# Pooled-attention kernel with adapters: key loads across 128 partitions and spread over the loop, first queries turned on TensorE, logits left in place, Exp without a bias tile

## The chip, the cores and the metric

The kernel runs on one core of one Trainium2 chip. The metric is the device time of one execution in microseconds (us). Times are medians of several executions, with the lowest and highest beside them. A run counts as slow when it is over 1.5% above the fastest of the same kernel. Ratios are the mean time of one kernel's fast runs over that of the other's fast runs of the same rounds, so they are not quite the ratio of the medians quoted.

Engines in the profile: PE is TensorE matmul, PEld its weight load, DVE VectorE, ACT ScalarE, POOL GpSimd, SP the sync engine, and a "q" at the end of a name (SPq, POOLq) is that engine's instruction queue, which also issues transfers.

## The reference

`q` is 4 x 12288 x 128, `kv` is 4 x 384 x 32 x 128, all float32. Keys and values are 4 x 4 averages of `kv`, projected: 768 of them per batch. Then eight adapters, of which the best two are used for every row.

```python
kv_pool = kv.reshape(B, H // 4, 4, W // 4, 4, C).mean(axis=(2, 4))
k = v = kv_pool.reshape(B, -1, C) @ w_sr
s = (q @ k.transpose(0, 2, 1)) / np.sqrt(C)
x = softmax(s) @ v                      # cut: written out with exp and sum
logits = x @ w_gate                     # 8 per row
topk = two largest logits per row;  w = softmax of those two
out = x + sum over the two of  w * (x @ A[e]) @ B[e]      # 16-wide adapters
```

## The kernel before

The kernel cuts the queries into 96 chunks of 512 rows, 24 per batch, and runs a software-pipelined loop with one chunk entering per round. I count rounds inside a batch with `i`, 0 to 23. Every round makes scores and Exp for one chunk, attends another (24 matmuls), normalizes a third, takes its top logits, and puts an older one through the adapters. Every fourth chunk ends a group, and its round also holds the "routing": four small DVE operations on the logits of the whole group. A chunk is normalized five rounds after it entered, so routing falls in rounds i = 8, 12, 16, 20 and, of the batch before, 0 and 4.

The keys of the next batch (6.3 MB) are fetched while the current batch is worked on, and their 4 x 4 sums are made by POOL, one small piece at a time. For the first batch they are made by DVE before the loop. These are the parts that the change and the argument touch (cuts are marked):

```python
def cast_q(g):            # POOL's queue: q group (2048 rows) to bfloat16 in DRAM
    keep(nc.gpsimd.dma_start(t, q[g // NG, (g % NG) * GT:(g % NG + 1) * GT]))
def load_qT(g):           # SP's queue: transposing load of that group
    keep(nc.sync.dma_start(t, q_bf[g], transpose=True))
def load_kv(b, l, xs, engines):        # 4 transfers, each into 32 partitions
    src = kv[b].rearrange("(hh hl r) (wh x) c -> wh hh hl r x c", hl=HL, r=4, x=WL * 4)
    for w in range(4):
        keep(engines[w % len(engines)].dma_start(
            kvr[b, l][32 * w:32 * w + 32, :, xs]...,  src[w, :, l, :, xs]...))
...
def top(k):               # per chunk
    for s in range(S):
        keep(nc.vector.max(srt[k0][:, m, s], xn[k][:, s, C:VC]))
    keep(nc.gpsimd.tensor_copy(lgs[k0][:, m], xn[k][:, :, C:VC]))    # logits, on POOL
def route(k0, step):      # per group of four chunks
    ... m12  = so[0] + so[1]            # DVE, both inputs in SBUF
    ... arg  = 2 * lg - m12             # DVE, both inputs in SBUF
    ... mask = lg >= so[1]              # DVE, both inputs in SBUF
def finish(k):            # osb = adapters' PSUM result + xn; 256 KB store on SP's queue
...
for k in range(LA, last + 2):          # the loop over rounds
    ...
        if i in (4, 5, 6):
            load_kv(b + 1, i - 4, slice(0, 2 * 4), [nc.sync])   # 4 x 512 KB at once
        if i >= 8:
            for _ in range(3):
                if sums:
                    sums.pop(0)()      # issues one key sum on POOL
    ...
```

The softmax here doesn't subtract the row's maximum and nothing guards it: scores larger than these inputs give would overflow.

Of the kernel before, what the change touches and what calls it, by code (L numbers as in the profile page):

```python
# [20 lines left out]
def kernel(  # L21
# [29 lines left out]
    kvpool = ctx.enter_context(tc.tile_pool(name="kvpool", bufs=4))  # L51
# [3 lines left out]
    xpool = ctx.enter_context(tc.tile_pool(name="xpool", bufs=9))  # L55
    rpool = ctx.enter_context(tc.tile_pool(name="rpool", bufs=3))
    run = ctx.enter_context(tc.tile_pool(name="run", bufs=3))
    opool = ctx.enter_context(tc.tile_pool(name="opool", bufs=4))
# [27 lines left out]
    HL, WL = 3, 2  # L86

    def load_kv(b, l, xs, engines):

        if (b, l) not in kvr:  # L90
            kvr[b, l] = kvpool.tile([P, 4, WL * 4, C], FP32, tag="kvr", name="kvr")
        src = kv[b].rearrange("(hh hl r) (wh x) c -> wh hh hl r x c", hl=HL, r=4, x=WL * 4)
        for w in range(4):
            keep(engines[w % len(engines)].dma_start(
                kvr[b, l][32 * w:32 * w + 32, :, xs].rearrange("p r x c -> p r (x c)"),
                src[w, :, l, :, xs].rearrange("p r x c -> p r (x c)")))

    w_sr_sb = const.tile([P, C], FP32)
# [3 lines left out]
    cast_q(0)  # L102
    for g in range(J):
        load_kv(0, g // WL, slice(4 * (g % WL), 4 * (g % WL) + 4), [nc.sync, nc.scalar])
        if g == 2:
            load_qT(0)
    a_f = const.tile([P, P], FP32)
    keep(nc.scalar.dma_start(a_f, moe_A.rearrange("e c r -> c e r")))
    b_f = const.tile([P, C], FP32)
    keep(nc.scalar.dma_start(b_f, moe_B.rearrange("e r c -> (e r) c")))  # L110



    shift = const.tile([P, 1], FP32)
    nc.vector.memset(shift, -0.25)
# [17 lines left out]
    def prepare(b, adder):  # L133
# [3 lines left out]
        def pool_step(g, step):  # L137
            l, w = g // WL, g % WL
            x = kvr[b, l][:, :, 4 * w:4 * w + 4]
            if step < 3:  # L140
                u, v = ((0, 1), (2, 3), (0, 2))[step]
                u, v = x[:, u], x[:, v]
            else:
                n = 2 if step == 3 else 1
                u, v = x[:, 0, 0:n], x[:, 0, n:2 * n]
            keep(adder.tensor_tensor(u, u, v, op=ALU.add))  # L146

        for g in range(J):
            for step in range(5):
                sums.append(lambda g=g, step=step: pool_step(g, step))  # L150
# [3 lines left out]
        def keys(h):  # L154
# [5 lines left out]
            for i in range(2):  # L160
                g = 2 * h + i
                mm(ps[:, i], kvr[b, g // WL][:, 0, 4 * (g % WL)], id_f,
                   is_transpose=True, start=(i == 0), stop=(i == 1))
# [26 lines left out]
    em, acc, xn, srt, gw = {}, {}, {}, {}, {}  # L190
# [3 lines left out]
    def scores(k, r):  # L194
# [7 lines left out]
        keep(nc.scalar.activation(em[k][:, 2 * r:2 * r + 2], ps, AF.Exp, bias=shift, scale=scale))  # L202
# [9 lines left out]
    def normalize(k):  # L212
        ri = rpool.tile([P, S], FP32, tag="rinv", name="rinv")
        keep(nc.vector.reciprocal(ri, acc[k][:, :, VC]))  # L214
        x = xpool.tile([P, S, VC], FP32, tag="xn", name="xn")
# [4 lines left out]
    lgs, rt = {}, {}  # L220
# [9 lines left out]
    def top(k):  # L230
        k0, m = first[k], k - first[k]
        if m == 0:
            srt[k0] = rpool.tile([P, GC, S, 8], FP32, tag="srt", name="srt")
            lgs[k0] = rpool.tile([P, GC, S, 8], FP32, tag="lgs", name="lgs")
        for s in range(S):
            keep(nc.vector.max(srt[k0][:, m, s], xn[k][:, s, C:VC]))  # L236
        keep(nc.gpsimd.tensor_copy(lgs[k0][:, m], xn[k][:, :, C:VC]))  # L237

    def route(k0, step):
        n = size[k0] * S  # L240
        lg = lgs[k0].rearrange("p m s e -> p (m s) e")[:, 0:n]
# [70 lines left out]
    for g in range(1, 3):  # L312
        cast_q(g)
    sums, rest = prepare(0, nc.vector)
    for h in range(3):
        for item in sums[10 * h:10 * h + 10] + rest[2 * h:2 * h + 2]:
            item()
        for k in range(LA):
            scores(k, h)
    for item in rest[6:]:  # L320
        item()
    a_bf = const.tile([P, P], BF16)
# [3 lines left out]
    load_qT(1)  # L326
# [9 lines left out]
    for k in range(LA, last + 2):  # L336
# [5 lines left out]
        if k % GC == 0:  # L342
            g = k // GC
            if g + 1 < B * NG and g + 1 not in qT:
                load_qT(g + 1)
            if g + 2 < B * NG and g + 2 not in q_bf:
                cast_q(g + 2)
        if b + 1 < B:
            if i == 4:
                sums, rest = prepare(b + 1, nc.gpsimd)  # L350
            if i in (4, 5, 6):
# [77 lines left out]
```

## Time and profile before

| | before |
|---|---|
| time | 515.11 us (512.03 to 515.84), three runs |
| PE busy | 411.9 us, 80% |
| first attended chunk normalized | 64.05 us |
| steady round | 3.835 us |

The first view is the page of the kernel before, span in 40 slices of 12.8 us; a digit is the busy share of a slice in tenths, and the last row is what the DMA engines moved.

```profile
PE   0025799899999954798999967589899999999973
DVE  0335348887888842887878854488778888888996
POOL 2000048760000063581000054275000100000000
DMA  9999999464464999954645899956446566552222
GB/s 232 177 174 210 207 206 242 107 146 90 110 131 104 206 235 225 195 112 120 124 98 127 171 234 222 219 108 147 97 105 136 108 144 150 126 104 65 83 83 82
```

PE is at 9 over most of the span, with three holes: the start, slices 15 to 17 counted from 1 (about 180 to 218 us) and slices 24 to 26 (about 295 to 333 us). In each hole the DMA engines are at 9 tenths while they move 174 to 242 GB/s. So there are three regimes: the start, the steady rounds and the reloads. The same in numbers, from busy time by stretch, kernel before (start:end and length in us, then busy time and instructions of PE, PEld, DVE, ACT and POOL, the TensorE clock that the chip granted as a share of full speed, DMA share, GB/s):

```profile
20.00:40.00 20.00, 4.04 (x8) 1.51 (x9) 9.38 (x18) 0.00 (x0) 0.00 (x0) 1.00 1.13 174
180.00:220.00 40.00, 23.89 (x244) 17.34 (x246) 21.03 (x55) 18.05 (x19) 22.13 (x28) 0.87 1.03 214
400.00:440.00 40.00, 39.44 (x468) 30.30 (x474) 34.02 (x103) 32.71 (x34) 3.58 (x13) 1.00 0.65 135
```

In the undisturbed stretch from 400 us PE is busy 39.4 of 40 us. In the reload stretch from 180 us it is busy 23.9.

The next two fences say what the holes are made of. The first is the timeline of the sync engine's queue in the kernel before (start, length, queue, line, operation, count): four key loads stand together, then stores, then a transposing q load.

```profile
178.86 8.35 SPq L94 DMA_DIRECT2D kvr<-in_kv_dram  x4
189.29 3.04 SPq L305 DMA_DIRECT2D out_dram<-osb  x2
194.08 11.69 SPq L83 DMA_TRANSPOSE qT<-qbf_2075  x1
```

The second is the view of waits (who waited, on what, total us, times, longest us): DVE waits for an output buffer because stores stand behind key loads, and for logits that POOL copies late because key sums stand ahead of them in POOL's queue.

```profile
DVE osb L304 <- DMA out_dram<-osb: 23.4, 4, 7.5
DVE arg L247 <- POOL lgs L237: 9.8, 2, 5.5
```

For the start, the timeline of the kernel before shows the last ten key sums on DVE and the first reciprocal (the first normalized chunk):

```profile
47.82 5.50 DVE L146 TENSOR_TENSOR kvr<-kvr 128x512 f32<-128x512 f32 x10
...
64.05 0.18 DVE L214 RECIPROCAL rinv<-acc 128x4 f32<-128x4 f32 x1 [2.49 <-PE acc L67]
```

Last, two groups of the page of the kernel before: the Exp (busy us, mean ns of one, idle before it) and the key loads (count, size, median us to landing).

```profile
L202 ACT ACTIVATE em<-sg,shift 128x1024 f16<-128x1024 f32 x288 | 306.8, 1111 | 112.1 <-PE sg L67 67.8
kvr<-in_kv_dram SPq DMA_DIRECT2D x36, 512.0 KB, 17.9
```

The trace's records of single transfers ("descriptors" below) add one more fact: a 4 KB piece of a key load took 329 ns (median) on one of the 16 DMA engines, a 2 KB piece of the start's loads 153 ns. That is 199 and 214 GB/s over 16 engines.

### The profile page before, as it was taken

Reading aid. Unit: us, or ns where it says so; the run is one execution under the profiler, and the core shown is the slowest. Engines: PE = TensorE matmul, PEld = TensorE weight load, DVE = VectorE, ACT = ScalarE, POOL = GpSimd, SP = SyncE. Lnnn points to the kernel's source line nnn. Section 1 sums busy time; section 2 is a strip of 40 time slices with the busy share of each in tenths; the row PEclk is TensorE's granted clock in tenths of the full one; section 3 lists DMA queues with packets and bytes.
Section 4 is the critical chain, followed back from the end, with each engine's and each line's share of the span. In section 5 each row is a group of like instructions: output and inputs, shape, how many; then the busy total and the mean of one; then the engine's idle time right before and its main releaser. Section 6 shows DMA issues by size and latency. Waiting matters only on the chain.

```text
span 512.7 us, 11238 instructions
## 1 busy us (share of the span) xinstructions
PE 411.9 (80%) x4444; PEld 302.6 (59%) x4515; DVE 362.4 (71%) x1048; ACT 313.2 (61%) x316; POOL 121.9 (24%) x216
## 2 busy tenths in 40 slices
PE   0025799899999954798999967589899999999973
PEld 0011467666767733576667755466676777777762
DVE  0335348887888842887878854488778888888996
ACT  0005798675778834586768855277667888788500
POOL 2000048760000063581000054275000100000000
PEclk9999899999999979899999997799999999999997
DMA  9999999464464999954645899956446566552222
GB/s 232 177 174 210 207 206 242 107 146 90 110 131 104 206 235 225 195 112 120 124 98 127 171 234 222 219 108 147 97 105 136 108 144 150 126 104 65 83 83 82
DMA packets 111541, 76.43 MB, mean 149 GB/s; under 512 B 54017, under 2 KB 103425, under 8 KB 111105
## 3 DMA queue, kind: packets, MB, share of 16 engines
q1 hardware_dynamic: 107520, 59.78, 52.9%
q0 software_dynamic: 768, 12.58, 14.3%
q10 hardware_dynamic: 3200, 3.35, 3.7%
q8 instruction: 35, 0.57, 0.5%
q14 instruction: 18, 0.14, 0.1%
HBM read 50.53 MB, written 37.75 MB: 172 GB/s over the span
## 4 chain that ended last, share of the span: by engine, by line
PE 39%; DVE 30%; DMA 18%; issue 7%; SPq 2%; POOL 2%; ACT 1%; DVEq 0%; POOLq 0%
PE acc L67 16%; DMA kvr<-in_kv_dram 11%; PE sg L67 9%; DVE xn L216 7%; DVE tts L277 6%; DMA out_dram<-osb 6%; PE d_ps L67 5%; PE tt_ps L67 4%; DVE hg L291 3%; PE h_ps L67 3%; DVE rinv L214 2%; DVE gw L259 2%; POOL kvr L146 1%; DMA b_f<-in_moe_B_dram 1%; SPq L83 1%
## 5 line engine op out<-in xcount | busy, mean ns | idle before, releaser
L202 ACT ACTIVATE em<-sg,shift 128x1024 f16<-128x1024 f32 x288 | 306.8, 1111 | 112.1 <-PE sg L67 67.8
L67 PE MATMUL acc<-vx,em 128*128 128x137 f16 x2304 | 178.0, 226 | 6.7 <-DVE xn L216 4.3
L67 PEld LDWEIGHTS <-em 128*128 128x128 f16 x2304 | 152.8, 99 | 39.3 <-DVE xn L216 32.4
L67 PE MATMUL sg<-qT,kfT 128*128 128x512 bf16 x505 | 162.2, 394 | 15.4 <-ACT em L202 7.5
L237 POOL COPY lgs<-xn 128x32 f32<-128x32 f32 x96 | 20.3, 211 | 366.8 <-DVE xn L216 366.5
L304 DVE TENSOR_TENSOR osb<-d_ps,xn 128x512 f32<-128x512 f32 x96 | 66.1, 689 | 38.8 <-DMA out_dram<-osb 23.4
L146 POOL TENSOR_TENSOR kvr<-kvr 128x512 f32<-128x512 f32 (+2 forms) x90 | 90.1, 1013 | 13.1 <-DMA kvr<-in_kv_dram 5.7
L67 PEld LDWEIGHTS <-tts 128*128 128x128 bf16 x768 | 52.6, 100 | 41.6 <-DVE tts L277 18.5
L216 DVE TENSOR_TENSOR xn<-acc,rinv 128x544 f32<-128x544 f32 x96 | 69.6, 725 | 3.3
L291 DVE TENSOR_TENSOR hg<-h_ps,gw 128x512 bf16<-128x512 f32 x96 | 66.2, 691 | 3.2 <-PE h_ps L67 0.6
L277 DVE COPY tts<-tt_ps 128x1024 bf16<-128x1024 bf16 (+1 forms) x99 | 65.9, 670 | 0.8 <-PE tt_ps L67 0.7
L67 PEld LDWEIGHTS <-kfT 128*128 128x128 bf16 x576 | 47.7, 100 | 26.4 <-issue 20.4
L67 PE MATMUL tt_ps<-id_bf,xn 128*128 128x128 bf16 x384 | 37.7, 221 | 28.7 <-DVE osb L304 24.7
L67 PEld LDWEIGHTS <-xn 128*128 128x128 bf16 x384 | 29.5, 98 | 50.5 <-issue 28.6
L67 PE MATMUL tt_ps<-id_bf,hg 128*128 128x128 bf16 x384 | 38.3, 224 | 9.6 <-DVE hg L291 9.6
L67 PE MATMUL d_ps<-b_bf,tts 128*128 128x128 bf16 x384 | 39.3, 227 | 4.4 <-DVE osb L304 1.1
L67 PE MATMUL h_ps<-a_bf,tts 128*128 128x128 bf16 x384 | 37.6, 221 | 1.3
L214 DVE RECIPROCAL rinv<-acc 128x4 f32<-128x4 f32 x96 | 17.1, 178 | 28.4 <-PE acc L67 28.3
L236 DVE MAX8 srt<-xn 128x8 f32<-128x8 f32 x384 | 34.9, 153 | 0.1
L67 PEld LDWEIGHTS <-hg 128*128 128x128 bf16 x384 | 25.0, 99 | 13.1 <-DVE hg L291 12.7
L251 ACT ACTIVATE th<-arg 128x128 f32<-128x128 f32 (+2 forms) x27 | 8.0, 298 | 39.6 <-DVE arg L247 30.4
L146 DVE TENSOR_TENSOR kvr<-kvr 128x512 f32<-128x512 f32 (+2 forms) x30 | 16.1, 556 | 15.3 <-DMA kvr<-in_kv_dram 14.6
(108 smaller groups left out, 106.4 us busy)
## 6 DMA issues: line engine op xcount, KB each, us to landing
out_dram<-osb SPq DMA_DIRECT2D x96, 256.0 KB, 2.7
kvr<-in_kv_dram SPq DMA_DIRECT2D x36, 512.0 KB, 17.9
kvr<-in_kv_dram SPq DMA_DIRECT2D x12, 256.0 KB, 10.4
kvr<-in_kv_dram ACTq DMA_DIRECT2D x12, 256.0 KB, 13.3
qbf_100<-in_q_dram POOLq DMA_DIRECT2D x1, 512.0 KB, 6.5
qbf_153<-in_q_dram POOLq DMA_DIRECT2D x1, 512.0 KB, 8.1
qbf_155<-in_q_dram POOLq DMA_DIRECT2D x1, 512.0 KB, 10.4
qbf_282<-in_q_dram POOLq DMA_DIRECT2D x1, 512.0 KB, 12.7
```

The source lines that it names most:

```text
L67: return keep(nc.tensor.matmul(*a, **k))
L146: keep(adder.tensor_tensor(u, u, v, op=ALU.add))
L202: keep(nc.scalar.activation(em[k][:, 2 * r:2 * r + 2], ps, AF.Exp, bias=shift, scale=scale))
L214: keep(nc.vector.reciprocal(ri, acc[k][:, :, VC]))
L216: keep(nc.vector.tensor_tensor(x, acc[k][:, :, 0:VC], ri.unsqueeze(2).broadcast_to([P, S, VC]), op=ALU.mult))
L236: keep(nc.vector.max(srt[k0][:, m, s], xn[k][:, s, C:VC]))
L237: keep(nc.gpsimd.tensor_copy(lgs[k0][:, m], xn[k][:, :, C:VC]))
L251: keep(nc.scalar.activation(th, arg, AF.Tanh, bias=0.0, scale=0.5))
L259: keep(nc.vector.scalar_tensor_tensor(w[:, 0:n], th, 1.0, mask, op0=ALU.add, op1=ALU.mult))
L277: keep(nc.vector.tensor_copy(sb[:, lo:hi], ps[:, lo:hi]))
L291: keep(nc.vector.tensor_tensor(hg[k].rearrange("p s (e r) -> p (s e) r", e=E), hp[k].rearrange("p s (e r) -> p (s e) r", e=E), gw[k0][:, m ...
L304: keep(nc.vector.tensor_tensor(osb, dp[k], xn[k][:, :, 0:C], op=ALU.add))
```

## The change

The intent is to shorten the start and the two reload holes. Six things change together: (1) key loads go to all 128 partitions in 1 KB runs, 256 KB each; (2) for later batches two of them are issued per round in rounds 4 to 15, not a burst in rounds 4 to 6; (3) q groups 0 and 1 are loaded as float32 and turned by TensorE, and the first casts wait until the start's loads have landed; (4) the logits stay in a group tile, so POOL's 96 copies go; (5) Exp has its bias as an immediate; (6) key sums are taken out two or three per round in rounds 9 to 20, one block of 256 keys per four rounds, and output buffers go from four to six. Two smaller things ride along: a first, empty Exp has ACT load its table (before, the load stood at 40.8 us), and the start's key loads no longer use ACT's queue. The core of the diff (cuts marked):

```diff
-    def load_kv(b, l, xs, engines):
-        ... four transfers of 32 partitions each ...
+    def load_kv(b, h, r, x):
+        src = kv[b, h * rows + r:(h + 1) * rows:4].rearrange("y (w k) c -> y w (k c)", k=4)
+        keep(nc.sync.dma_start(kvr[b, h][:, r, x], src[:, :, x * 2 * C:(x + 1) * 2 * C]))
+    def turn_q(g, m, engine):
+        ... four TensorE transposes of float32 q, one copy from PSUM to bf16 ...
-    cast_q(0)
-    ... 24 key loads on the SP and ACT queues, load_qT(0) among them ...
+    load_q(0, 0, GC * S)
+    for h in range(3):
+        for r in range(4):
+            for x in range(2):
+                load_kv(0, h, r, x)
+    for m in range(GC):
+        load_q(1, m * S, m * S + S)
...
-        keep(nc.scalar.activation(em..., ps, AF.Exp, bias=shift, scale=scale))
+        keep(nc.scalar.activation(em..., ps, AF.Exp, bias=0.0, scale=scale))
...
-        keep(nc.gpsimd.tensor_copy(lgs[k0][:, m], xn[k][:, :, C:VC]))
-        lg = lgs[k0].rearrange("p m s e -> p (m s) e")[:, 0:n]
+        lg = xg[k0].rearrange("p m s c -> p (m s) c")[:, 0:n, C:VC]
...
+    keep(nc.gpsimd.tensor_copy(late, q_f[1][:, GC * S - 1, 0:1]))   # casts wait for this
...
-            if i in (4, 5, 6):
-                load_kv(b + 1, i - 4, slice(0, 2 * 4), [nc.sync])
-            if i >= 8:
-                for _ in range(3): ... sums.pop(0)()
+            if 4 <= i < 16:
+                h, j = divmod(i - 4, 4)
+                load_kv(b + 1, h, j, 0)
+                load_kv(b + 1, h, j, 1)
+            if 9 <= i < 21:
+                h, j = divmod(i - 9, 4)
+                for _ in range(3 if j == 3 else 2):
+                    if sums[h]:
+                        sums[h].pop(0)()
```

More of the change, by code (lines that the diff above doesn't have):

```diff
@@ L50 @@
     prep = ctx.enter_context(tc.tile_pool(name="prep", bufs=1))
-    kvpool = ctx.enter_context(tc.tile_pool(name="kvpool", bufs=4))
+    kvpool = ctx.enter_context(tc.tile_pool(name="kvpool", bufs=3))
     per_b = ctx.enter_context(tc.tile_pool(name="per_b", bufs=2))
@@ L54 @@
     ppool = ctx.enter_context(tc.tile_pool(name="ppool", bufs=7))
-    xpool = ctx.enter_context(tc.tile_pool(name="xpool", bufs=9))
+    xpool = ctx.enter_context(tc.tile_pool(name="xpool", bufs=4))
     rpool = ctx.enter_context(tc.tile_pool(name="rpool", bufs=3))
     run = ctx.enter_context(tc.tile_pool(name="run", bufs=3))
-    opool = ctx.enter_context(tc.tile_pool(name="opool", bufs=4))
+    opool = ctx.enter_context(tc.tile_pool(name="opool", bufs=6))
     qdram = ctx.enter_context(tc.tile_pool(name="qdram", bufs=1, space=bass.MemoryType.DRAM))
@@ L84, in load_qT, with load_q @@
         qT[g] = t
-    HL, WL = 3, 2
-    def load_kv(b, l, xs, engines):
-        if (b, l) not in kvr:
-            kvr[b, l] = kvpool.tile([P, 4, WL * 4, C], FP32, tag="kvr", name="kvr")
-        src = kv[b].rearrange("(hh hl r) (wh x) c -> wh hh hl r x c", hl=HL, r=4, x=WL * 4)
-        for w in range(4):
-            keep(engines[w % len(engines)].dma_start(
-                kvr[b, l][32 * w:32 * w + 32, :, xs].rearrange("p r x c -> p r (x c)"),
-                src[w, :, l, :, xs].rearrange("p r x c -> p r (x c)")))
+    def load_kv(b, h, r, x):
+        if (b, h) not in kvr:
+            kvr[b, h] = kvpool.tile([P, 4, 2, 2, 2 * C], FP32, tag="kvr", name="kvr")
+        rows = H // 3
+        src = kv[b, h * rows + r:(h + 1) * rows:4].rearrange("y (w k) c -> y w (k c)", k=4)
+        keep(nc.sync.dma_start(kvr[b, h][:, r, x], src[:, :, x * 2 * C:(x + 1) * 2 * C]))
+    def load_q(g, lo, hi):
+        if g not in q_f:
+            q_f[g] = xpool.tile([P, GT // P, C], FP32, tag="xn", name="qf")
+        r = slice(g * GT + lo * P, g * GT + hi * P)
+        keep(nc.sync.dma_start(q_f[g][:, lo:hi], q[0, r].rearrange("(s p) c -> p s c", p=P)))
+    def turn_q(g, m, engine):
+        if m == 0:
+            qT[g] = qpool.tile([P, GT], BF16, tag="qT", name="qT")
+        ps = mtile([P, S, P], name="qT_ps")
+        for i in range(S):
+            mm(ps[:, i], q_f[g][:, m * S + i], id_f, is_transpose=True,
+               start=(i == 0), stop=(i == S - 1))
+        o = qT[g][:, m * T:(m + 1) * T].rearrange("p (s t) -> p s t", s=S)
+        if engine is nc.scalar:
+            keep(nc.scalar.copy(o, ps))
+        else:
+            keep(nc.vector.tensor_copy(o, ps))
+    q_f = {}
     w_sr_sb = const.tile([P, C], FP32)
@@ L101 @@
     keep(nc.scalar.dma_start(w_gate_sb, moe_w_gate))
-    cast_q(0)
-    for g in range(J):
-        load_kv(0, g // WL, slice(4 * (g % WL), 4 * (g % WL) + 4), [nc.sync, nc.scalar])
-        if g == 2:
-            load_qT(0)
-    a_f = const.tile([P, P], FP32)
-    keep(nc.scalar.dma_start(a_f, moe_A.rearrange("e c r -> c e r")))
-    b_f = const.tile([P, C], FP32)
-    keep(nc.scalar.dma_start(b_f, moe_B.rearrange("e r c -> (e r) c")))
-    shift = const.tile([P, 1], FP32)
-    nc.vector.memset(shift, -0.25)
+    load_q(0, 0, GC * S)
[5 more added lines that the diff above has]
+        load_q(1, m * S, m * S + S)
+    b_f = const.tile([P, C], FP32)
+    keep(nc.sync.dma_start(b_f, moe_B.rearrange("e r c -> (e r) c")))
+    a_f = const.tile([P, P], FP32)
+    keep(nc.sync.dma_start(a_f, moe_A.rearrange("e c r -> c e r")))
+    warm = const.tile([P, 1], FP32)
+    nc.vector.memset(warm, 0.0)
+    keep(nc.scalar.activation(warm, warm, AF.Exp, bias=0.0, scale=1.0))
     id_f = const.tile([P, P], FP32)
@@ L135, in prepare, with pool_step @@
         sums, rest = [], []
-        def pool_step(g, step):
-            l, w = g // WL, g % WL
-            x = kvr[b, l][:, :, 4 * w:4 * w + 4]
+        def pool_step(h, step, lo, hi):
+            t = kvr[b, h]
             if step < 3:
-                u, v = ((0, 1), (2, 3), (0, 2))[step]
-                u, v = x[:, u], x[:, v]
-            else:
-                n = 2 if step == 3 else 1
-                u, v = x[:, 0, 0:n], x[:, 0, n:2 * n]
-            keep(adder.tensor_tensor(u, u, v, op=ALU.add))
-        for g in range(J):
-            for step in range(5):
-                sums.append(lambda g=g, step=step: pool_step(g, step))
+                u, v = t[:, 0].rearrange("p x g c -> p (x g c)"), t[:, step + 1].rearrange("p x g c -> p (x g c)")
+            elif step == 3:
+                u, v = t[:, 0, 0].rearrange("p g c -> p (g c)"), t[:, 0, 1].rearrange("p g c -> p (g c)")
+            else:
+                u, v = t[:, 0, 0, :, 0:C], t[:, 0, 0, :, C:2 * C]
+                keep(adder.tensor_tensor(u, u, v, op=ALU.add))
+                return
+            keep(adder.tensor_tensor(u[:, lo:hi], u[:, lo:hi], v[:, lo:hi], op=ALU.add))
+        for h in range(3):
+            block = []
+            for step in range(5):
+                if adder is nc.vector:
+                    n = w = 1024 if step < 3 else 512
+                else:
+                    n, w = 1024 if step < 3 else 512, 512
+                for lo in range(0, n, w):
+                    block.append(lambda h=h, step=step, lo=lo, w=w: pool_step(h, step, lo, lo + w))
+            sums.append(block)
         st = {}
@@ L160, in keys @@
             for i in range(2):
-                g = 2 * h + i
-                mm(ps[:, i], kvr[b, g // WL][:, 0, 4 * (g % WL)], id_f,
+                mm(ps[:, i], kvr[b, h][:, 0, 0, i, 0:C], id_f,
                    is_transpose=True, start=(i == 0), stop=(i == 1))
@@ L187, in prepare @@
         return sums, rest
-    em, acc, xn, srt, gw = {}, {}, {}, {}, {}
+    em, acc, xn, xg, srt, gw = {}, {}, {}, {}, {}, {}
     tts, xT, hgT, hp, hg, dp = {}, {}, {}, {}, {}, {}
@@ L201, in scores @@
             mm(ps[:, i], kfT[b][:, 2 * r + i], rhs, start=True, stop=True)
-        keep(nc.scalar.activation(em[k][:, 2 * r:2 * r + 2], ps, AF.Exp, bias=shift, scale=scale))
+        keep(nc.scalar.activation(em[k][:, 2 * r:2 * r + 2], ps, AF.Exp, bias=0.0, scale=scale))
     def attend(k, s):
@@ L214, in normalize @@
         keep(nc.vector.reciprocal(ri, acc[k][:, :, VC]))
-        x = xpool.tile([P, S, VC], FP32, tag="xn", name="xn")
+        k0, m = first[k], k - first[k]
+        if m == 0:
+            xg[k0] = xpool.tile([P, GC, S, VC], FP32, tag="xn", name="xn")
+        x = xg[k0][:, m]
         keep(nc.vector.tensor_tensor(x, acc[k][:, :, 0:VC],
@@ L218, in normalize @@
         xn[k] = x
-    lgs, rt = {}, {}
+    rt = {}
     sizes = [GC] * (NCHUNK // GC - 2) + [2, 2, 2, 1, 1]
@@ L233, in top @@
             srt[k0] = rpool.tile([P, GC, S, 8], FP32, tag="srt", name="srt")
-            lgs[k0] = rpool.tile([P, GC, S, 8], FP32, tag="lgs", name="lgs")
         for s in range(S):
             keep(nc.vector.max(srt[k0][:, m, s], xn[k][:, s, C:VC]))
-        keep(nc.gpsimd.tensor_copy(lgs[k0][:, m], xn[k][:, :, C:VC]))
     def route(k0, step):
         n = size[k0] * S
-        lg = lgs[k0].rearrange("p m s e -> p (m s) e")[:, 0:n]
+        lg = xg[k0].rearrange("p m s c -> p (m s) c")[:, 0:n, C:VC]
         so = srt[k0].rearrange("p m s e -> p (m s) e")[:, 0:n]
@@ L310 @@
     LA = 4
-    for g in range(1, 3):
-        cast_q(g)
+    for m in range(GC):
+        turn_q(0, m, nc.scalar)
     sums, rest = prepare(0, nc.vector)
     for h in range(3):
-        for item in sums[10 * h:10 * h + 10] + rest[2 * h:2 * h + 2]:
+        for item in sums[h] + rest[2 * h:2 * h + 2]:
             item()
@@ L321 @@
         item()
+    late = const.tile([P, 1], FP32)
+    keep(nc.gpsimd.tensor_copy(late, q_f[1][:, GC * S - 1, 0:1]))
+    for g in range(2, 4):
+        cast_q(g)
     a_bf = const.tile([P, P], BF16)
@@ L325 @@
     keep(nc.vector.tensor_copy(b_bf, b_f))
-    load_qT(1)
+    turn_q(1, 0, nc.scalar)
     enter = {}
@@ L343 @@
             g = k // GC
-            if g + 1 < B * NG and g + 1 not in qT:
+            if 2 <= g + 1 < B * NG:
                 load_qT(g + 1)
-            if g + 2 < B * NG and g + 2 not in q_bf:
+            if 4 <= g + 2 < B * NG and g + 2 not in q_bf:
                 cast_q(g + 2)
@@ L350 @@
                 sums, rest = prepare(b + 1, nc.gpsimd)
-            if i in (4, 5, 6):
-                load_kv(b + 1, i - 4, slice(0, 2 * 4), [nc.sync])
-            if i >= 8:
-                for _ in range(3):
-                    if sums:
-                        sums.pop(0)()
+            if 4 <= i < 16:
[7 more added lines that the diff above has]
+                        sums[h].pop(0)()
         if ks:
@@ L364 @@
             transposes(x_, h_)
+        if k + 1 in range(GC + 1, 2 * GC):
+            turn_q(1, (k + 1) % GC, nc.scalar)
         if ks:
```

## The prediction

> **What bounds the kernel now.** Three regimes, read from busy time by stretch.
> (1) Start: PE is busy 2 tenths or less until 35 us; the DMA share is near 1.0 at only 144 to 225 GB/s. The timeline has the last key sums at 47.8 to 52.6 us, released by key loads, and the first reciprocal of an attended chunk at 64.0 us. Until then 6.3 MB of keys, each transfer into 32 partitions, compete with four q casts and two DMA transposes.
> (2) Steady state: the chain of waits gives one attend group per 3.835 us per chunk of 512 rows (411.5, 415.4, 419.2 us); PE is busy 19.7 of 20 us, ACT 16.4, DVE 17. PE binds.
> (3) Key reloads for batches 2 and 3: in 180-220 us PE is busy 23.9 of 40 us, and ACT runs 19 instructions where steady stretches have 33; in 300-340 us 25.9 and 20. About 4.5 chunks are lost each time: 18 + 17 = 35 us. The waits name causes: the sync queue issues 12 key loads of 512 KB in a burst, and output stores queue behind them (DVE osb waits 23.4 us for stores, 4 times); routing logits wait behind key sums in POOL's in-order queue (9.8 us, twice).
>
> **What the change does.**
> - Keys go to 128 partitions in 1 KB runs. The Trainium skill ("SBUF — State Buffer", Door 1) says 32 partitions reach 8 of 16 DMA ports (189 against 328 GB/s at 1 MiB). The trace agrees on the first half: a 4 KB key descriptor took 329 ns median, 199 GB/s over 16 engines; the fastest tenth of 2 KB ones took 84 ns. Estimate for 1 KB: 45 ns, about 350 GB/s, so 6.3 MB in 18 us.
> - q groups 0 and 1 are loaded plain (1 MB each; 512 B store descriptors took 27 ns, so 3.5 us) and turned on TensorE: 32 fp32 transposes at 0.27 to 0.47 us, 8 ACT copies, about 0.6 us each. Casts wait until the start's loads landed.
> - Estimate for the start: 2 + 3.5 + 18 us, keys landed near 24 us instead of 48; last sum to first reciprocal 11.5 us as before, plus 1: first reciprocal near 40 us. Gain 24 us. The q turns in the first loop rounds give back 1.5 us on ACT.
> - Reloads: two 256 KB loads per chunk over 12 chunks instead of a burst; stores interleave, osb has 6 buffers, logits skip POOL. DMA demand per chunk, by descriptor times: stores 0.9, transposes 0.65, cast 0.8, keys 1.45 us: 3.8 of 3.84 us. Just fits; I expect 2 us of waiting per reload. Gain about 30 of 35 us.
> - Exp without bias tile: the skill ("ScalarE: Activation LUTs", What ACT_TABLE_LOAD costs) gives 93 ns per pointer operand; 1111 ns should become about 1020. ACT is not the limit: almost nothing, as for the 96 POOL copies (0.21 us each).
> - Unchanged: steady pace, the 7.6 us per batch of key projections, the DVE-bound tail.
>
> **Predicted time:** 515.1 - 24 + 1.5 - 30 = 462 us; 8 in 10 between 450 and 476. Faster by over 2%: 0.97, within: 0.02, slower: 0.01.
>
> **What would show it:** first reciprocal at 37 to 44 us; 1 KB key descriptors at 40 to 55 ns; no 20 us stretch between 60 and 440 with PE below 16; no wait of osb for stores over 2 us; pace still 3.83.
>
> **What would make it wrong:** DMA saturated during reloads, so q transposes land late and PE waits (near 480); 1 KB loads no faster than 220 GB/s (start gain only 12 us); POOL sums late for the projections.

## The result, and the profile after

The changed kernel took 465.26 us (463.83 to 468.69); the kernel before, in the same rounds, 514.51 (512.03 to 515.84). The ratio is 0.906, 95% interval 0.899 to 0.912, and the output is correct. The profiled runs have spans of 512.7 and 462.2 us, so 50.5 us went.

The page of the kernel after, in 40 slices of 11.6 us:

```profile
PE   4578998989999988979999988978999999999872
DVE  2752588878688888878788888897788888888995
POOL 0011734810000835720000537450000000000000
DMA  8998949985237978996145899999234244422222
GB/s 279 377 221 201 214 137 216 260 184 119 71 90 196 253 215 225 254 203 142 47 115 126 251 246 230 256 194 207 70 94 115 69 115 116 109 75 70 70 92 91
```

The holes are filled, and the second slice moved 377 GB/s. Busy time by stretch, kernel after, same columns as before:

```profile
20.00:40.00 20.00, 15.20 (x44) 6.29 (x44) 10.37 (x17) 10.86 (x12) 2.03 (x4) 0.55 0.95 217
180.00:220.00 40.00, 34.89 (x388) 25.71 (x393) 33.38 (x93) 25.68 (x28) 11.71 (x13) 1.00 0.83 193
```

In 180 to 220 us PE is now busy 34.9 of 40 us, against 23.9. The times of the 96 reciprocals, one per round, say where the 50.5 us came from. The "excess" is what a batch's 24 rounds take above 24 x 3.835 us:

| | before | after | gain |
|---|---|---|---|
| first reciprocal at | 64.05 | 44.20 | 19.8 |
| excess, batch 0 | 10.5 | 10.7 | -0.2 |
| excess, batch 1 | 28.9 | 13.8 | 15.0 |
| excess, batch 2 | 29.3 | 14.0 | 15.3 |
| excess, batch 3 | 4.8 | 4.4 | 0.5 |
| last reciprocal to the end | 10.8 | 10.8 | 0.0 |

(Gains were taken before rounding.) So the start gave 20 us and each of two reloads 15. The disturbed rounds of batch 1 were "11.0 7.0 10.5" us before. After, what stands out is each routing round: 5.9, 5.5 and 6.3 us in batch 1, where batch 3, which loads no keys, has 4.1. The key projections (rounds "5.6 5.6 4.4 4.6 5.0 5.0 4.1", 7.5 us above the pace) are the same in both kernels.

The start, in the timeline of the kernel after: the sums of the three key blocks on DVE, each followed by two evictions, then the first reciprocal.

```profile
9.93 4.68 DVE L167 TENSOR_TENSOR kvr<-kvr 128x1024 f32<-128x1024 f32 x4 [5.45 <-DMA kvr<-in_kv_dram]
...
17.67 0.42 DVE L198 CAST kfT<-kfT_ps 128x256 bf16<-128x256 f32 x1 [1.38 <-PE kfT_ps L67]
18.01 4.46 DVE L167 TENSOR_TENSOR kvr<-kvr 128x1024 f32<-128x1024 f32 x4
...
25.79 4.46 DVE L167 TENSOR_TENSOR kvr<-kvr 128x1024 f32<-128x1024 f32 x4
...
44.20 0.18 DVE L241 RECIPROCAL rinv<-acc 128x4 f32<-128x4 f32 x1 [3.88 <-PE acc L67]
```

The second and third blocks waited for no load (no idle time stands behind their lines): after 9.9 us the start is bound by DVE's order of work (sums, then standing while PE projects the keys, then evictions), not by transfers.

One thing beside the change moved the start: the granted clock. Here is the same stretch of the kernel after, then of e3_logits, a run below that starts in the same way:

```profile
20.00:30.00 10.00, 7.69 (x17) 2.08 (x15) 7.70 (x10) 5.92 (x7) 2.03 (x4) 0.50 1.04 271
20.00:30.00 10.00, 6.77 (x17) 1.78 (x15) 8.44 (x11) 6.83 (x8) 1.96 (x3) 0.83 1.05 279
```

Over 14 to 44 us the mean clock was 0.60 or 0.61 in five profiles that start in this way (after, after_again, f3_later, e6_nosums, e7_shift), with the first reciprocal at 43.9 to 44.3 us, and 0.89 in three others (e3_logits, e5_bias, f1_sched), with 42.3 to 42.9; e1_burst, at 0.77, had 43.9. So 1 to 2 us of a start go with the clock. What set it was not tested, and differences of 2 us between first reciprocals are not read as effects.

The two groups shown of before, now after:

```profile
L229 ACT ACTIVATE em<-sg 128x1024 f16<-128x1024 f32 x288 | 284.2, 1021 | 120.9 <-PE sg L67 87.2
kvr<-in_kv_dram SPq DMA_DIRECT2D x96, 256.0 KB, 4.8
```

A key load lands in 4.8 us instead of 17.9; its 1 KB pieces took 46 ns (median), which is 356 GB/s over 16 engines. The last keys of the start landed at 23.2 us instead of 46.4. Over the whole run, the engine time of all key pieces fell from 120.8 to 78.8 us of 16 engines. DVE no longer waits for stores.

What makes a routing round long is in the timeline of the kernel after, one routing round of batch 1 (m is the sum of the two best logits):

```profile
160.25 1.45 DVE L273 TENSOR_TENSOR m_2420<-srt 128x16 f32<-128x16 f32 x1
160.37 1.28 POOL L167 TENSOR_TENSOR kvr<-kvr 128x512 f32<-128x512 f32 x1
161.72 0.73 POOL L165 TENSOR_TENSOR kvr<-kvr 128x256 f32<-128x256 f32 x1
161.74 0.87 DVE L275 SCALAR_TENSOR_TENSOR arg<-xn,m_2420 128x128 f32<-128x128 f32 x1
163.46 0.38 PE L67 MATMUL tt_ps<-id_bf,xn 128*128 128x128 bf16 x4 [0.86 <-DVE osb L332]
```

A sum of 16 x 128 numbers took 1.45 us, as long as the POOL key sum beside it, and `arg` 0.87 us beside the next; undisturbed they take 0.19 and 0.29. DVE works in order, so the output addition behind them is late, and PE stands for 0.86 us. That is what the Trainium skill ("SBUF — State Buffer", Who interferes with whom) says of a DVE instruction with two SBUF inputs and a GpSimd instruction that reads SBUF: one holds the shared read port for its whole length and the other waits. The same was there before the change (`arg` up to 1.23 us), but hidden under larger losses. The next section tests whether this, or the DMA engines, which are at 0.99 to 1.02 share in 80 to 100, 160 to 180 and 280 to 300 us, is what is left.

### The profile page after: what moved, and what is told of

It is laid out like the page before. It is cut to its first block, busy times and chain, and to the rows that moved or that the text cites. A ratio compares the mean times of both kernels' runs of the same rounds, so it can differ in the third digit from the quotient of the medians.

```text
span 462.2 us, 11209 instructions
## 1 busy us (share of the span) xinstructions
PE 406.1 (88%) x4475; PEld 302.1 (65%) x4547; DVE 364.9 (79%) x1033; ACT 295.6 (64%) x325; POOL 97.0 (21%) x101
## 4 chain that ended last, share of the span: by engine, by line
PE 43%; DVE 31%; issue 5%; DVEq 0%
PE acc L67 17%; PE sg L67 10%; DVE xn L246 8%; DVE tts L305 7%; PE d_ps L67 5%; PE h_ps L67 4%; DVE hg L319 3%; PE tt_ps L67 3%; DVE mask L281 3%; DVE gw L287 2%; DVE srt L265 1%; DVE rinv L241 1%; PE kfT_ps L67 1%; PE v_ps L67 1%; DVE kfT L198 1%
## 5 line engine op out<-in xcount | busy, mean ns | idle before, releaser
L229 ACT ACTIVATE em<-sg 128x1024 f16<-128x1024 f32 x288 | 284.2, 1021 | 120.9 <-PE sg L67 87.2
L67 PE MATMUL acc<-vx,em 128*128 128x137 f16 x2304 | 174.9, 224 | 8.3 <-DVE xn L246 5.4
L67 PEld LDWEIGHTS <-em 128*128 128x128 f16 x2304 | 150.1, 98 | 36.6 <-DVE xn L246 30.6
L67 PE MATMUL sg<-qT,kfT 128*128 128x512 bf16 x504 | 159.7, 390 | 3.9 <-ACT em L229 1.6
L167 POOL TENSOR_TENSOR kvr<-kvr 128x512 f32<-128x512 f32 x63 | 78.7, 1272 | 183.4 <-PE tt_ps L67 57.9
L67 PEld LDWEIGHTS <-tts 128*128 128x128 bf16 x768 | 51.2, 98 | 41.3 <-DVE tts L305 19.1
L67 PE MATMUL tt_ps<-id_bf,hg 128*128 128x128 bf16 x384 | 37.3, 220 | 7.6 <-DVE hg L319 7.6
L265 DVE MAX8 srt<-xn 128x8 f32<-128x8 f32 x384 | 34.9, 154 | 0.1
L167 DVE TENSOR_TENSOR kvr<-kvr 128x1024 f32<-128x1024 f32 (+1 forms) x12 | 13.1, 1090 | 6.0 <-DMA kvr<-in_kv_dram 5.4
L207 DVE CAST vx<-v_ps 128x408 f16<-128x408 f32 x8 | 4.7, 584 | 12.1 <-PE v_ps L67 12.0
```

Of the source, the lines that this page charges most:

```text
L67: return keep(nc.tensor.matmul(*a, **k))
L167: keep(adder.tensor_tensor(u[:, lo:hi], u[:, lo:hi], v[:, lo:hi], op=ALU.add))
L229: keep(nc.scalar.activation(em[k][:, 2 * r:2 * r + 2], ps, AF.Exp, bias=0.0, scale=scale))
```

## The experiments

My theory: the start's gain comes from the key layout; the reloads' gain comes from narrow bursts becoming wide, spread loads; what is left of a reload is POOL's sums beside DVE's routing. Rivals: TensorE's turning of q made the start; pacing alone, or layout alone, made the reloads; the rest is DMA saturation; the logits or the bias contributed.

Twelve runs were made, one of them a repeat of the kernel after, all beside the kernel before (medians 512.65 to 514.95 us over four groups). "Excess" is of batches 0, 1, 2.

| run | what | median (range) us | ratio to before | excess, profiled run |
|---|---|---|---|---|
| e1_burst | after, loads in bursts | 494.28 (475.62 to 536.2) | none, one fast run | 10.4 / 31.9 / 19.3 |
| e2_half | after, 64 partitions | 479.11 (474.75 to 481.43) | 0.932 | 15.7 / 16.8 / 16.4 |
| e3_logits | after, POOL copies kept | 463.86 (462.67 to 464.64) | 0.904 | 11.1 / 12.9 / 12.9 |
| e4_qdma | after, q by cast and DMA | 468.44 (467.73 to 469.14) | 0.912 | 10.5 / 16.0 / 16.7 |
| b1_paced | before, loads spread | 493.77 (479.85 to 507.44) | none, one fast run | 9.3 / 15.6 / 21.4 |
| e6_nosums | after, no POOL sums (wrong result) | 483.5 (483.01 to 483.66) | 0.940 | see text |
| e7_shift | after, loads three rounds later | 455.98 (451.36 to 459.97) | 0.880 | 10.7 / 10.4 / 13.5 |
| e8_actkeys | after, start's evictions on ACT | 464.81 (461.65 to 467.16) | 0.904 | not used |
| f1_sched | e3_logits, sums moved | 477.55 (476.79 to 479.2) | 0.931 | 17.0 / 17.4 / 17.7 |
| e5_bias | after, bias tile kept | 468.45 (465.86 to 471.07) | 0.912 | not used |
| after_again | after, unchanged | 467.51 (466.42 to 469.82) | 0.912 | 14.0 / 14.6 / 15.6 |
| f3_later | f1_sched, one round later | 449.98 (448.48 to 450.66) | 0.876 | 6.7 / 8.8 / 8.8 |

The changed kernel itself repeated as 465.26, then 467.51; differences of 3 us between groups of runs are not read as effects.

### e1_burst: wide loads in a burst

```diff
-            if 4 <= i < 16:
-                h, j = divmod(i - 4, 4)
-                load_kv(b + 1, h, j, 0)
-                load_kv(b + 1, h, j, 1)
+            if i in (4, 5, 6):
+                for j in range(4):
+                    load_kv(b + 1, i - 4, j, 0)
+                    load_kv(b + 1, i - 4, j, 1)
```

> The kernel after, but the key loads of the next batch go out in three rounds of eight transfers again (wide 1 KB-run layout kept, 6 output buffers kept, no POOL logits). Theory P (pacing is what saved the reloads): output stores queue behind 2 MB bursts as before and most of the 30 us come back, 481 to 495 us. Theory L (the wide layout makes the burst short: 24 transfers at about 46 ns per 1 KB descriptor are 18 us, and six output buffers cover 23 us): 461 to 471 us. My own guess: +6 us, from q transposes that land late behind the burst.

The best of four runs was 475.6 us, about 10 above the changed kernel; the others were 486.8, 501.8 and 536.2, while runs of the kernel before in between stayed within 0.9% of each other. The best run lies between the two ranges expected. Three of four count as slow, and the profiled run is a slow one. Its waits show the kind of loss, a transposing q load that lands late:

```profile
PE sg L67 <- DMA qT<-qbf: 27.1, 3, 20.0
```

In that trace POOL also issued six q casts between 158 and 182 us, during the burst and right after it; whether the key loads or these casts held the q load up is not separated. Either way, spreading the loads is needed also with the wide layout, and what it buys first is steadiness.

### e2_half: 64 partitions per transfer

```diff
-        keep(nc.sync.dma_start(kvr[b, h][:, r, x], src[:, :, x * 2 * C:(x + 1) * 2 * C]))
+        keep(nc.sync.dma_start(kvr[b, h][64 * x:64 * x + 64, r]...,      # same 256 KB,
+            src[:, x * n:(x + 1) * n].rearrange("y (w e) -> y w e", w=2)))   # 4 KB runs
```

(The sums' operand shapes follow the new layout.)

> The kernel after with the same number and size of key transfers, but each goes into 64 partitions (in runs of 4 KB[...]) instead of 128. If the number of DMA ports reached is the cause of the fast loads, descriptors run at half the rate (about 330 ns or more per 4 KB, against 4 x 46 = 184 ns), keys land about 13 us later and the first reciprocal comes 8 to 12 us later than 44.2 us; reloads get up to 10 us longer each: 475 to 500 us. If the layout is not the cause (no competing casts, pacing alone), 463 to 468 us.

479.11 us: 14 us of the gain went. The first reciprocal came at 50.0 us, 5.8 later (8 to 12 expected), the last keys of the start landed at 32.7 us instead of 23.2, and every batch lost 2 to 5 us. A 4 KB piece took 255 ns; four 1 KB pieces of the wide layout take 184. The Trainium skill ("SBUF — State Buffer", Door 1) says that 64 partitions reach no more DMA ports than 32 do, 196 against 189 GB/s. Here the 64-partition pieces ran at 257 GB/s over 16 engines (16 x 4096 B / 255 ns) and the 32-partition pieces of the kernel before at 199, with other traffic beside both. So a loss against 128 partitions is there (257 against 356 GB/s), and smaller than in the page's rates of single transfers. This tests the layout as a whole, not the ports alone: the runs were of 4 KB, not 1 KB, and transfers into both halves of the partitions were under way at a time.

### e3_logits: POOL's logits copies kept

```diff
+        keep(nc.gpsimd.tensor_copy(lgs[k0][:, m], xn[k][:, :, C:VC]))
-        lg = xg[k0].rearrange("p m s c -> p (m s) c")[:, 0:n, C:VC]
+        lg = lgs[k0].rearrange("p m s e -> p (m s) e")[:, 0:n]
```

> The kernel after with the 96 POOL copies of the routing logits put back, everything else kept. If the copies behind key sums in POOL's in-order queue cost what the waits of before showed (9.8 us) or more, 472 to 480 us. If pacing already spread the key sums so that a copy waits for one sum of 1.3 us at most, 464 to 469 us; q casts should then be issued at an even pace again instead of in advance, since each copy holds POOL's queue to the pace of the chunks.

463.86 us with a spread of 2 us: removing the copies won nothing. The routing rounds of batches 0 to 2 were all 5.4 to 5.5 us where the changed kernel had 4.4 to 6.9. The trace shows why it is steadier: a copy waits for the round's DVE work, so in POOL's in-order queue it also holds back what comes after it. Without the copies POOL ran ahead of the loop, and q casts went out in bunches (at 93.0, 93.5 and 94.0 us in the kernel after, where the loop asks for one per group of four rounds).

### e4_qdma: q groups 0 and 1 by cast and DMA transpose

```diff
-    load_q(0, 0, GC * S)
+    cast_q(0)
+    cast_q(1)
...
+        if h == 2:
+            load_qT(0)
-        load_q(1, m * S, m * S + S)      # and the turn_q calls taken out
+    load_qT(1)
```

> The kernel after with q groups 0 and 1 brought in as before (cast to DRAM by POOL's DMA, then DMA transpose), the wide key layout kept. If taking casts and transposes off the start was a real part of the gain, the first reciprocal comes at 50 to 56 us instead of 44.2 and the time is 471 to 478 us. If the start is bound by the chain of sums and projections on DVE (last sums at 25.8 to 30.7 us, when the loads had landed), it is 464 to 468 us.

468.44 us, just above the second range, and the first reciprocal at 44.56 us against 44.20. The bulk of the start's gain does not come from turning q on TensorE. It is not without effect, though. With the casts and the transposing load beside them the last keys landed at 29.8 us instead of 23.2, and the last sums ended at 32.8 instead of 30.7; from there to the first reciprocal it took 11.7 us instead of 13.5, with no q group to turn on the way. And this start had the higher clock (0.89 over 14 to 44 us), at which the kernels that turn q had 42.3 to 42.9 us: turning q may be worth some 2 us of the 20.

### b1_paced: the kernel before with its loads spread

```diff
-            if i in (4, 5, 6):
-                load_kv(b + 1, i - 4, slice(0, 2 * 4), [nc.sync])
-            if i >= 8:
-                for _ in range(3):
-                    if sums:
-                        sums.pop(0)()
+            if 4 <= i < 16:          # load_kv now takes a list of the quarters to load
+                l, w = divmod(i - 4, 4)
+                load_kv(b + 1, l, slice(0, 2 * 4), [nc.sync], [w])
+            if 9 <= i < 21:
+                for _ in range((3, 3, 3, 1)[(i - 9) % 4]):
+                    sums.pop(0)()
```

> The kernel before with one edit: its 12 key loads per batch (512 KB into 32 partitions each) go out one per round over 12 rounds instead of four per round over 3, and the key sums follow them. The start and everything else stay. If pacing is what saved the reloads, the two stalls of 15 us in batches 1 and 2 (8 to 11 us rounds) shrink to 3 us or less each and the time is 484 to 491 us. If the narrow transfers still saturate the DMA, or the logits behind key sums stall it, it stays above 500 us.

One run at 479.85 us, the others 489.7 to 507.4 (slow); 484 to 491 was expected. The start was as before (first reciprocal 61.7 us in the profiled run), and batches 1 and 2 lost 15.6 and 21.4 us instead of 28.9 and 29.3. Pacing can bring most of the reloads' gain without the wide layout, but a round of 10.0 or 12.3 us still turns up. Neither e1_burst nor b1_paced gave a kernel whose runs agree, so pacing is needed, and so is something else of the change. That this is the layout is argued, not shown: b1_paced also keeps four output buffers (DVE waited for stores twice, 3.9 us in all).

### e6_nosums: no key sums on POOL (wrong result)

```diff
                 sums, rest = prepare(b + 1, nc.gpsimd)
+                sums = [[], [], []]
```

> The kernel after without the key sums on POOL for batches 1 to 3 (only the first of the 16 pixels is used: wrong result on purpose), all transfers kept. Theory S (the routing operations of DVE wait while POOL adds, since both read two operands from SBUF): the rounds of 5.5 to 6.9 us at the end of a group fall to 4.1 us, the mask operation to 0.28 us, and the time falls by 12 to 15 us to 450 to 453 us. Theory D (those rounds are long because the DMA is saturated, share 0.99 to 1.02): within 2 us of 465 us.

Slower: 483.5 us. In batches 1 and 2 the expectation of my theory held: every routing round took 4.1 us, and the excess was 8.4 in both, with all key loads still running. But a round of batch 0 took 38.8 us. With neither copies nor sums, nothing held POOL's queue back: all 22 casts were issued between 27 and 66 us, and a transposing load came late:

```profile
PE sg L67 <- DMA qT<-qbf: 32.6, 1, 32.6
```

The total is therefore no measure of the sums; the rounds are. The side effect fits what e3_logits suggested, that POOL's work also set the pace of its queue.

### e7_shift: loads three rounds later, sums one round earlier

```diff
-            if 4 <= i < 16:
-                h, j = divmod(i - 4, 4)
+            if 7 <= i < 19:
+                h, j = divmod(i - 7, 4)
...
-            if 9 <= i < 21:
-                h, j = divmod(i - 9, 4)
-                for _ in range(3 if j == 3 else 2):
+            if 8 <= i < 20:
+                h, j = divmod(i - 8, 4)
+                for _ in range(2):
```

> The kernel after with the key loads of the next batch three rounds later (rounds 7 to 18 instead of 4 to 15), so that the sums, which POOL runs as soon as the keys land, fall between two routing rounds. No work is taken away. Theory S: most of the collisions go, -8 to -14 us, 451 to 457 us. Theory D: same bytes over the same number of rounds, within 2 us of 465 us. It could lose if the last block's sums come too late for its projections in round 20.

The fast runs took 451.36 and 453.38 us, two others 458.57 and 459.97. In the profiled one (slow) the first two routing rounds of each batch took 3.7 to 4.1 us, and the third 7.3, 5.7 and 7.8. Moving the sums moved the loss with them. But sums that start when data lands sit where the transfers put them, so the time varies.

### e8_actkeys: the start's two evictions on ACT

```diff
+            if b == 0:
+                keep(nc.scalar.activation(kpT..., ps, AF.Copy, bias=0.0, scale=1.0 / 16.0))
+            else: ...          # the DVE instruction as before; the same for kfT
```

> The kernel after with the two PSUM evacuations of the first batch's key projections on ACT instead of DVE. If the start is bound by DVE, which stands still 2 x 2.95 us for the projections between blocks of sums while the keys have landed, the last sums end at 25 to 27 us instead of 30.7, the first reciprocal comes 3 to 5 us earlier (39 to 41 us) and the time is 460 to 463 us. If the DMA bounds the start, nothing moves.

The last key sums ended at 26.4 us instead of 30.7, but the first reciprocal came at 41.5, only 2.7 earlier, because the projections then queued behind scores and Exps (the last block's began 2.9 us after its last sum). Even the 2.7 us are not all the edit's: this run had the full clock throughout its start, and e3_logits, at 0.89, has 42.3. The total, 464.81 us, can't be told from the changed kernel. DVE's order did bind the sums; behind it stands the next limit.

### f1_sched: sums placed around the routing, a miss

```diff
+ ... POOL's logits copies kept, as in e3_logits ...
-                for _ in range(3 if j == 3 else 2):
-                    if sums[h]:
-                        sums[h].pop(0)()
+                for _ in range((3, 3, 2, 0)[j]):
+                    sums[h].pop(0)()
```

> The kernel after with the POOL logits copies back (they hold POOL's queue to the pace of the rounds, as the run with them showed) and the eight key sums of a block put as 3, 3, 2 and 0 into the four rounds of a group, none into the routing round. Theory S (DVE's two-operand routing operations wait for POOL's sums): the nine long routing rounds of 5.5 us fall to 4.2 us each, mask 0.28 us, and the time falls by 11 to 13 us against the kernel with copies (463.9) to 451 to 454 us, with little spread, since casts are paced too. Theory D (DMA saturated): 462 to 466 us.

477.55 us: 13.7 slower than e3_logits, not faster. I had the round wrong by one. A sum taken out in round i stands in POOL's queue behind the copy of round i-1, so those of rounds 9, 13 and 17 ran in the routing rounds 8, 12 and 16. The timeline of f1_sched, one routing round:

```profile
182.45 3.77 POOL L167 TENSOR_TENSOR kvr<-kvr 128x512 f32<-128x512 f32 x3
...
183.15 0.61 DVE L275 TENSOR_TENSOR m<-srt 128x16 f32<-128x16 f32 x1
183.86 1.23 DVE L277 SCALAR_TENSOR_TENSOR arg<-lgs,m 128x128 f32<-128x128 f32 x1
185.01 1.35 DVE L283 TENSOR_TENSOR mask<-lgs,srt 128x128 f32<-128x128 f32 x1
```

All three DVE operations now ran beside sums, and routing rounds took 6.6 us (one 6.4). It is a clean test all the same: same transfers, same sums, only their place differs. And the sizes add up. In e3_logits two sums fall beside a routing, here three, in f3_later below none, and the rounds take 5.5, 6.6 and 4.2 us. Here `m` is stretched by 0.42 us, `arg` by 0.94 and `mask` by 1.07: together 2.4 us, all of 6.6 - 4.2. In these three traces no `m`, `arg` or `mask` without a sum beside it took over 0.29 us.

### e5_bias and after_again: the bias of Exp, and a repeat

```diff
+    shift = const.tile([P, 1], FP32)
+    nc.vector.memset(shift, -0.25)
-    ... AF.Exp, bias=0.0, scale=scale))
+    ... AF.Exp, bias=shift, scale=scale))
```

> The kernel after with the Exp bias as a [128,1] tile again. Exp should take 1111 ns instead of 1021; ACT is not the limit in the loop, so the time stays within 1.5 us of the kernel after in the same rounds. If the shorter Exp mattered for PE (its waits for sg buffers), it is 5 us or more slower.

> The kernel after, unchanged, as the control of these rounds: 463 to 469 us.

468.45 us with the bias tile, 467.51 without, in the same rounds, ranges overlapping: 90 ns less for each of 288 Exps brings nothing that can be seen, since ACT is not the limit.

### f3_later: the same schedule one round later (diff against f1_sched)

```diff
-            if 9 <= i < 21:
-                h, j = divmod(i - 9, 4)
+            if 10 <= i < 22:
+                h, j = divmod(i - 10, 4)
```

> One line away from the run with the mis-set schedule (477.6): the key sums of the changed kernel, with the logits copies on POOL kept, are taken out of the queue one round later, in batch rounds 10 to 12, 14 to 16 and 18 to 20, three, three and two at a time. The off-by-one is mended: a sum taken out in round i runs behind the logits copy of round i-1, so nothing should now run on POOL beside the routing of rounds 8, 12 and 16. Theory (POOL key sums beside the DVE routing ops with two SBUF operands are what is left of the reload cost): all routing rounds of batches 0 to 2 go to about 4.2 us, from 5.5 in the run with only the logits copies put back (463.9) and 6.6 in the mis-set one; the excess per batch falls to 9 to 10 us, and the time to 450 to 454 us, with a spread under 3 us. Rival (what is left is DMA saturation while keys are reloaded): the lost time moves to other rounds and the total stays 460 to 466 us. A second miss of the schedule (sums again beside routing) would show as mask and arg instructions over 1 us and POOL sums at the same time.

449.98 us (448.48 to 450.66), correct, ratio 0.876 (0.873 to 0.880) to the kernel before. Only the round in which the sums are taken out differs from f1_sched, by one, and 27.6 us went. The timeline of f3_later (DVE and POOL of a routing round, and the round after it):

```profile
171.85 0.19 DVE L275 TENSOR_TENSOR m<-srt 128x16 f32<-128x16 f32 x1
172.14 0.29 DVE L277 SCALAR_TENSOR_TENSOR arg<-lgs,m 128x128 f32<-128x128 f32 x1
172.35 0.28 DVE L283 TENSOR_TENSOR mask<-lgs,srt 128x128 f32<-128x128 f32 x1
...
175.31 3.72 POOL L167 TENSOR_TENSOR kvr<-kvr 128x512 f32<-128x512 f32 x3
176.17 0.69 DVE L334 TENSOR_TENSOR osb<-d_ps,xn 128x512 f32<-128x512 f32 x1 [0.21 <-PE d_ps L67]
```

The routing is alone and quick. The sums run beside `osb`, whose inputs are one in PSUM and one in SBUF, and `osb` takes its usual 0.69 us: sums cost nothing there. The routing rounds 8, 12 and 16 took 3.7 to 4.2 us in every batch. Against the DMA rival stands the busy time by stretch of f3_later (same columns as before):

```profile
160.00:180.00 20.00, 19.56 (x233) 15.06 (x236) 16.81 (x54) 15.22 (x17) 15.00 (x18) 1.00 1.05 266
```

With DMA engines fully busy (1.05) PE still works 19.56 of 20 us; the changed kernel, at a share of 1.02 in the same stretch, has 18.14. A second profile of f3_later agrees: 19.41 us at a share of 1.02 in 180 to 200 us. The same key loads are there as in the changed kernel, in the same rounds. This version beats both kernels: 450.0 us against 465.3 and 514.5.

## Why the prediction was right or wrong

**Total: right.** 462 us predicted, 450 to 476 as the range; 465.26 measured.

**Start: the gain was 19.8 us, not 24; the transfers were right, the time from the last landing to the first reciprocal was mis-sized.** 1 KB pieces took 46 ns against the 45 estimated, and the last keys landed at 23.2 us against "near 24 us". Two terms behind that were too small. First, "near 40 us" leaves some 3.5 us from the last landing to the last sum; it took 7.5. DVE works on sums and evictions in order: from 9.9 us on, three blocks of about 5 us of sums, and 2.9 us of standing and evicting after each of the first two, end at 30.7 us. Second, "last sum to first reciprocal 11.5 us as before, plus 1" took 13.5 (10.7 in the kernel before, by its trace). Some 1.4 us more went into q turns: from the end of the value evictions (`vx`) to the first reciprocal it took 4.1 us, before and in e4_qdma 2.7 to 2.8. About another 1.3 go with the clock: the same way took 12.2 us in e3_logits. So the first reciprocal came at 44.2 us, just outside the 37 to 44 that I had asked for; in e3_logits, at the higher clock, it came at 42.3.

**Turning q: 1.5 us predicted as a loss in the first loop rounds; some 1.4 us seen, but before the first reciprocal.** The excess of batch 0 (-0.2) does not show it. e4_qdma shows that turning q was not needed for the bulk of the start's gain.

**Reloads: the gain of 30 us was right (15.0 and 15.3), but two terms of it were mis-sized and cancelled.** I read 18 + 17 us as lost before. By reciprocals, batches 1 and 2 lost 28.9 and 29.3 us; less the 8.8 that f3_later keeps (7.5 of them the key projections), that is 20.1 and 20.5. I expected "2 us of waiting per reload" to stay. What stayed, above the same floor, is 13.8 - 8.8 = 5.0 and 14.0 - 8.8 = 5.2 us. So the loss was read 5.6 us too small and the rest 6.2 us too small; that their difference came out right is luck. And the cause of the rest was not the one I gave: "DMA demand ... just fits" pointed at the DMA engines. They were full (share 0.99 to 1.02), but what stayed was POOL's sums beside DVE's routing. e6_nosums, f1_sched and f3_later show it, each by rounds, f3_later also by the total. The prediction names POOL's sums only as possibly late for the projections; it does not ask what runs beside them.

**Logits and Exp: "almost nothing" was right** (e3_logits, e5_bias). Exp went from 1111 to 1021 ns, near the 93 ns that the Trainium skill ("ScalarE: Activation LUTs", What ACT_TABLE_LOAD costs) gives for a pointer operand. I had not foreseen that the copies paced POOL's queue.

**The other checks held:** no 20 us stretch from 60 to 440 us has PE below 16 us (lowest 16.03, in 300 to 320), DVE waits for no store, the pace is 3.835 us. The danger that I named, q transposes late behind saturated transfers, came true only in variants, above all in e1_burst (20.0 us at most) and e6_nosums (32.6).

**Open:** of the 19.8 us of the start, runs of the changed kernel give back 5.8 (64 partitions) and perhaps 2 (q not turned); loads into 32 partitions were not put back, so that the rest comes from the layout is argued from the landing of the last keys (46.4 to 23.2 us). Why the first reload, in batch 0, cost little before the change (excess 10.5) was not tested. Nor was the new schedule without the logits copies, so how much of f3_later's steadiness comes from them is argued from e3_logits, e6_nosums and e7_shift, not shown alone. The two more output buffers were never tested apart from the rest, and what set the clock of the start is not known.

## What to carry to other kernels

Load wide and spread the loads evenly over the loop: in this kernel a version without the one and a version without the other each had single rounds of 10 us or more and runs that did not agree. An engine that is mostly idle can still cost time by what runs beside it, so place its work by the round in which it will really run, and check that in the trace: one round's shift was worth 27.6 us. Before you call a few microseconds of a start an effect, look at the granted clock of that stretch. Before removing a cheap instruction from an in-order queue, ask whether it is what holds that queue in step with the loop.

## What the Trainium skill lacked or had wrong

- "SBUF — State Buffer", Door 1: the page gives rates for transfers of 1 MiB by partition count, and none for runs of 1 KB. Here runs of 1 KB into 128 partitions took 46 ns per DMA engine (356 GB/s over 16), and loads of 256 KB (keys and q) queued behind each other moved 377 GB/s in a slice of 11.6 us, where "The DMA setup-cost knee" of the same page has 224 GB/s for a transfer of 256 KiB. That figure is of one transfer alone.
- The same section calls 64 partitions as slow as 32 (196 against 189 GB/s). In these runs pieces of 64-partition loads ran at 257 GB/s and those of 32-partition loads at 199, and 128 partitions at 356. Other traffic ran beside all three, and transfers into different partitions were under way at a time, so this does not refute the page's rates of single transfers.
- "SBUF — State Buffer", Who interferes with whom: the rule held. A DVE operation of 0.19 to 0.29 us took up to 1.65 us beside a POOL sum of 1.27 us, and with one input in PSUM stayed at 0.69 us; a different place of the same sums moved the kernel from 477.6 to 450.0 us.
- I found no page that warns that an in-order queue can run ahead of the loop when cheap instructions are taken out of it: with all of POOL's loop work gone, one q transpose was waited for by 32.6 us (e6_nosums).
- I found no page that says how bursts of loads spread the times of single runs: 475.6 to 536.2 us for one kernel (e1_burst), where the spread version stayed within 463.8 to 468.7.
